# Queries and keys turned by DVE in squares of 32, scores in the array's four row groups

## The chip, the core and the metric

The kernel runs on one core of one Trainium2 chip. The metric is the device time of one execution in microseconds. The kernel before was timed in three executions: median 586.64 us, 584.97 to 586.91 us. A profiled execution (span 578.5 us on the core, TensorE at 0.971 of its full clock on average) gives the times of single instructions. Engines are named as the profile names them: PE is TensorE's matrix multiply, PEld its weight load, DVE is VectorE, ACT is ScalarE, POOL is GpSimd, SP the engine that issues most of the DMA. PSUM is the memory into which PE writes, in banks of 2 KB a partition; SBUF is the working memory of 128 partitions.

## The reference

Two blocks in a row, all in fp32: an attention with a local window and a few global keys, and a layer of eight experts of which each token uses one.

```python
# attention: q, k, v are (4 batches, 8 heads, 768 positions, 64)
scores = q @ k.T / 8                        # per batch and head
keep = (key < n_global) | (0 <= query - key < n_local)     # n_global 8, n_local 96
bias = -slope[h] * dist                     # dist = query - key, or n_local for a far global key
a = softmax(where(keep, scores + bias, -1e9))
x = (a @ v)                                 # heads side by side: 3072 tokens x 512
# router and experts
logits = normed(x) @ normed(expert_emb).T / tau
e = argmax(logits); gate = softmax(logits)[e]
out = gate * (relu(x @ w1[e]) @ w2[e])      # w1 512 x 1024, w2 1024 x 512
```

## The kernel before

The attention goes by groups: a batch and four of its heads (8 groups, two a batch). A group has eight blocks of 96 keys; the keys of a block are seen by its own 96 queries and by the next 96, and 30 further rows hold the possible global keys. So scores of a block are 126 keys by 192 queries a head, keys in the partitions. A step takes two blocks (a group has 4 steps, the kernel 32).

For the scores, PE contracts over the head dimension, so q and k must lie with that dimension in the partitions. They are loaded by tokens: 128 tokens in the partitions, two heads side by side, in runs of 256 bytes. PE turns them with an identity matrix into PSUM, and ACT copies the result out.

```python
def load_tokens(eng, dst, src, b, a, r0, r1):          # two heads (a pair): 256-byte runs
    for e in range(2):
        eng.dma_start(dst[:, r0:r1, e, :],
                      src[b, 2 * a + e].rearrange("(t p) d -> p t d", p=P)[:, r0:r1, :])

def turn(t, i):                                        # a half of q or k of a pair
    src, half = (t.k, t.q)[i // 2], i % 2
    ps = bank()                                        # one of five PSUM banks, shared in turn
    for r in range(3):
        nc.tensor.transpose(ps[:, r * P : (r + 1) * P], src[:, 3 * half + r, :, :], k.ident[:])   # L399
    if i < 2:
        nc.scalar.copy(out=t.kT[:, 4 * half : 4 * half + 4, 0:BLK], ...)     # L401
    else:
        nc.scalar.copy(out=t.qT[:, 3 * half * P : 3 * (half + 1) * P], ...)  # L404
    if i == 0:   # the global keys beside each block
        nc.scalar.copy(out=t.kT[:, :, BLK:ROWS], in_=t.kT[:, 0:1, 0:GLB].to_broadcast([P, NB, GLB]))  # L406

def score(u):                                          # one block u, four heads; L418
    u.sp = [bank() for _ in range(2)]
    for a in range(2):                                 # pair of heads
        for e in range(2):                             # head of the pair: partitions 0-63 or 64-127
            rows = slice(e * D, (e + 1) * D)
            nc.tensor.matmul(u.sp[e][0:ROWS, a * n : (a + 1) * n], lhsT=t.kT[rows, j, 0:ROWS],
                             rhs=t.qT[rows, j * BLK : j * BLK + n], start=True, stop=True)

def grow(u, e):                                        # ACT: exp(scale * scores) into SBUF; L422
    ...
def weigh(u):                                          # DVE: ex = ex * table (bias and mask); L429
    ...
def attend(g, p):                                      # PE: ex x v (L444), sums over the keys (L452)
    ...
    if p % 2:                                          # every second step: out of PSUM
        nc.scalar.copy(out=xd[:, 1, :], ...)           # L457
        nc.vector.tensor_copy(out=xd[:, 0, :], ...)    # L458
        ... den: nc.vector.tensor_copy (L463) for the first group of a batch, nc.vector add (L465) for the second
```

The steps, shortened. Each engine runs its instructions in the order in which they are written here:

```python
for s, (g, p) in enumerate(steps):
    ...                                    # loads of q, k, v two groups ahead
    for u in us: score(u)                  # us: the two blocks of the step
    grow(us[0], 0); grow(us[0], 1)
    weigh(us[0])
    grow(us[1], 0)
    turn(...)                              # turns[s]: two or so a step, of the group ahead
    grow(us[1], 1)
    ...                                    # the other turns; then, for the batch before:
    for hf in active: half_turns(hf)       # PE turns x (L516), DVE scales it (xs, L521), ACT squares it (L526),
                                           # routing: den turned (L483), products lh, lg (L506, L508), small DVE work
    weigh(us[1])
    attend(*steps[s - 1])                  # one step behind
    ...                                    # expert scores (L492), weights of the first experts by DMA
```

After the attention come the experts (L968 is x by w1, L904 by w2), with rows gathered and scattered by GpSimd's indirect DMA (L881, L908).

Of the kernel before, what the change touches and what calls it, by code (L numbers as in the profile page):

```python
# [9 lines left out]
F32 = mybir.dt.float32  # L10
# [10 lines left out]
P = 128  # L21
# [264 lines left out]
def window_table(k, tmp):  # L286

# [33 lines left out]
    for m in range(2):  # L323
        yield
        for e in range(2):
            for a in range(2):
                nc.scalar.activation(k.table[:, m, e, a], rel[:], AF.Exp, scale=-k.slopes[4 * m + 2 * a + e])
# [3 lines left out]
def window_attention(k, ctx):  # L331

# [4 lines left out]
    def pool(name, bufs, **kw):  # L337
# [6 lines left out]
                 for name, n in (("wa_qk", 4), ("wa_tmp", 1)))  # L344
    kt_p, v_p = pool("wa_kt", 4), pool("wa_v", 3)
    ex_p, late_p, const = pool("wa_ex", 6), pool("wa_late", 2), pool("wa_const", 1)
    xd_p, den_p, xs_p, rt_p = pool("wa_xd", 5), pool("wa_den", 3), pool("wa_xs", 2), pool("wa_rt", 2)
    k.junk = const.tile([P, k.DM], F32, name="junk")
    k.table = const.tile([P, 2, 2, 2, 4, BLK], F32, name="table")
# [6 lines left out]
    def new_pair():  # L356
        t = Net()
        t.k = qk_p.tile([P, NT, 2, D], F32, name="k", tag="k")
        t.q = qk_p.tile([P, NT, 2, D], F32, name="q", tag="q")
        t.qT = kt_p.tile([P, S], F32, name="qT", tag="qT")  # L360
        t.kT = kt_p.tile([P, NB, P], F32, name="kT", tag="kT")
        return t

    def load_tokens(eng, dst, src, b, a, r0, r1):

        for e in range(2):
            eng.dma_start(dst[:, r0:r1, e, :],
                          src[b, 2 * a + e].rearrange("(t p) d -> p t d", p=P)[:, r0:r1, :])
# [12 lines left out]
    def open_group(g):  # L381
        g.pairs = [new_pair() for _ in range(2)]
        g.v = v_p.tile([P, 4, NB, D], F32, name="v", tag="v")

    def load_part(g, p):
        if p < 2:
            load_tokens(nc.sync, g.pairs[p].k, k.k, g.b, 2 * g.m + p, 0, NT)
            load_tokens(nc.sync, g.pairs[p].q, k.q, g.b, 2 * g.m + p, 0, NT)
        else:
            load_v(g, (2 * p - 4, 2 * p - 3))  # L390
# [3 lines left out]
    def turn(t, i):  # L394

        src, half = (t.k, t.q)[i // 2], i % 2
        ps = bank()
        for r in range(3):
            nc.tensor.transpose(ps[:, r * P : (r + 1) * P], src[:, 3 * half + r, :, :], k.ident[:])  # L399
        if i < 2:  # L400
            nc.scalar.copy(out=t.kT[:, 4 * half : 4 * half + 4, 0:BLK],  # L401
                           in_=ps[:, 0 : 3 * P].rearrange("d (j c) -> d j c", c=BLK))
        else:
            nc.scalar.copy(out=t.qT[:, 3 * half * P : 3 * (half + 1) * P], in_=ps[:, 0 : 3 * P])  # L404
        if i == 0:
            nc.scalar.copy(out=t.kT[:, :, BLK:ROWS], in_=t.kT[:, 0:1, 0:GLB].to_broadcast([P, NB, GLB]))  # L406

    def score(u):

        j, n = u.j, u.n  # L410
        u.sp = [bank() for _ in range(2)]
        u.ex = (late_p if u.late else ex_p).tile([P, 2, 2, 2 * BLK], F32, name="ex", tag="ex")
        u.ex = u.ex[0:ROWS, :, :, 0:n]
        for a in range(2):
            t = u.g.pairs[a]
            for e in range(2):
                rows = slice(e * D, (e + 1) * D)
                nc.tensor.matmul(u.sp[e][0:ROWS, a * n : (a + 1) * n], lhsT=t.kT[rows, j, 0:ROWS],  # L418
                                 rhs=t.qT[rows, j * BLK : j * BLK + n], start=True, stop=True)

    def grow(u, e):
        nc.scalar.activation(u.ex[:, e], u.sp[e][0:ROWS, 0 : 2 * u.n].rearrange("p (a c) -> p a c", a=2), AF.Exp,  # L422
                             scale=k.scale)
# [766 lines left out]
```

## Time and profile before

| view | what it shows |
|---|---|
| median time | 586.64 us (3 executions) |
| span of the profiled execution | 578.5 us, 9188 instructions |
| PE busy | 548.2 us (95%), 3542 matmuls |
| DVE, ACT busy | 164.5 us (28%), 142.3 us (25%) |
| score matmuls (L418), 64x192 and 64x96 | 512, mean 336 ns |
| turns of q and k on PE (L399) | 96 and 96, mean 299 and 292 ns |
| their copies on ACT (L401, L404) | 32 and 32, mean 498 and 484 ns |
| products with the window's table on DVE (L429), 126x768 | 56, mean 954 ns |
| copies of 128x384 on DVE: xd (L458), den (L463) | 16 and 8, mean 550 and 546 ns |
| DMA packets | 117331, of which 92965 are under 512 bytes |

How to read it: in the profile's lists, a line such as "L418 PE MATMUL pa<-qT,kT 64*126 64x192 f32" is a group of instructions of line 418: the engine, the operation, the tile written and those read, the rows and columns of the array that are used (64 rows, 126 columns), and the moving operand's shape. Matmuls overlap in the array, so their mean durations add up to more than the time they take; the distance between their starts is the cost of one. "Busy" is the time in which at least one instruction ran on that engine. The DMA share is the busy share of the core's 16 DMA engines.

### The profile page before, as it was taken

Reading aid. Unit: us, or ns where it says so; the run is one execution under the profiler, and the core shown is the slowest. Engines: PE = TensorE matmul, PEld = TensorE weight load, DVE = VectorE, ACT = ScalarE, POOL = GpSimd, SP = SyncE. Lnnn points to the kernel's source line nnn. Section 1 sums busy time; section 2 is a strip of 40 time slices with the busy share of each in tenths; the row PEclk is TensorE's granted clock in tenths of the full one; section 3 lists DMA queues with packets and bytes.
Section 4 is the critical chain, followed back from the end, with each engine's and each line's share of the span. In section 5 each row is a group of like instructions: output and inputs, shape, how many; then the busy total and the mean of one; then the engine's idle time right before and its main releaser. Section 6 shows DMA issues by size and latency. Waiting matters only on the chain.

```text
span 578.5 us, 9188 instructions
## 1 busy us (share of the span) xinstructions
PE 548.2 (95%) x3542; PEld 350.8 (61%) x3542; DVE 164.5 (28%) x411; ACT 142.3 (25%) x336; POOL 101.8 (18%) x130
## 2 busy tenths in 40 slices
PE   8899999999989798999999999999999999999980
PEld 8577788787767676757444447556556444645530
DVE  3254666675775412111000110212101110210010
ACT  4575756756643210001001001001001001001100
POOL 2000015013232225140130013030130130110010
PEclk9799999999989898999999999999999999999995
DMA  8999998994246414543460326443461460010000
GB/s 174 194 186 201 258 254 182 256 235 72 74 128 185 126 25 129 189 150 115 177 238 0 123 84 238 158 142 120 160 232 39 159 226 30 16 43 20 2 36 25
DMA packets 117331, 78.11 MB, mean 135 GB/s; under 512 B 92965, under 2 KB 101157, under 8 KB 117169
## 3 DMA queue, kind: packets, MB, share of 16 engines
q1 hardware_dynamic: 109744, 60.72, 40.9%
q0 software_dynamic: 5536, 15.25, 7.4%
q8 instruction: 51, 0.84, 0.6%
q14 instruction: 112, 0.91, 0.5%
q10 hardware_dynamic: 1888, 0.40, 0.4%
HBM read 63.38 MB, written 13.16 MB: 132 GB/s over the span
## 4 chain that ended last, share of the span: by engine, by line
PE 58%; issue 2%; DMA 1%; POOL 1%; DVE 0%; POOLq 0%
PE big L968 27%; PE work L904 25%; PE work L939 3%; PE work L894 2%; DMA xg<-x_dram,ids 1%; POOL xg L881 0%; POOL out_dram L908 0%; POOL meta L245 0%; DVE y L907 0%; POOLq L1004 0%; DVE flags L1018 0%; POOLq L908 0%; POOLq L881 0%
## 5 line engine op out<-in xcount | busy, mean ns | idle before, releaser
L968 PE MATMUL big<-xT,w1t 128*128 128x320 f32 (+5 forms) x512 | 159.0, 472 | 0.0
L904 PE MATMUL work<-w2t,hT 128*128 128x512 f32 x320 | 139.4, 595 | 0.0
L968 PEld LDWEIGHTS big<-xT,w1t 128*128 128x128 f32 x512 | 95.0, 193 | 64.4 <-issue 31.6
L904 PEld LDWEIGHTS work<-w2t,hT 128*128 128x128 f32 x320 | 60.3, 190 | 74.6 <-issue 73.8
L970 ACT ACTIVATE hT<-big 128x640 f32<-128x640 f32 (+5 forms) x32 | 24.9, 777 | 303.7 <-PE big L968 303.7
L429 DVE TENSOR_TENSOR ex<-ex,table 126x768 f32<-126x768 f32 x64 | 57.7, 904 | 57.9 <-ACT ex L422 55.9
L907 DVE TENSOR_SCALAR y<-work,emt 128x512 f32<-128x512 f32 x22 | 16.5, 751 | 156.7 <-PE work L904 150.0
L422 ACT ACTIVATE ex<-pa 126x384 f32<-126x384 f32 (+1 forms) x128 | 53.3, 476 | 28.8 <-PE pa L418 28.8
L908 POOL DMA_INDIRECT out_dram<-y,ids x22 | 21.8, 992 | 185.6 <-DVE y L907 133.1
L895 DVE COPY xT<-work 128x512 f32<-128x512 f32 x32 | 20.1, 683 | 109.9 <-PE work L894 109.9
L418 PE MATMUL pa<-qT,kT 64*126 64x192 f32 (+1 forms) x512 | 50.7, 336 | 0.4 <-ACT ex L422 0.4
L444 PE MATMUL od<-ex,v 126*64 126x192 f32 (+1 forms) x576 | 48.6, 316 | 0.0
L418 PEld LDWEIGHTS pa<-qT,kT 64*126 64x126 f32 x512 | 41.5, 190 | 10.7 <-issue 6.0
L444 PEld LDWEIGHTS od<-ex,v 126*64 126x64 f32 x576 | 36.0, 142 | 8.8 <-issue 4.7
L881 POOL DMA_INDIRECT xg<-x_dram,ids x34 | 33.3, 981 | 23.0 <-issue 15.6
L245 POOL DMA_INDIRECT meta<-mt,slot x24 | 26.3, 1095 | 38.3 <-DVE good L542 7.8
L452 PE MATMUL od<-ex,halves 126*32 126x192 f32 (+1 forms) x576 | 26.9, 310 | 0.0
L943 POOL DMA_INDIRECT out_dram<-y,pids x7 | 7.1, 1015 | 89.3 <-DVE y L942 84.0
L217 POOL TENSOR_TENSOR ss<-ss,half 128x3 f32<-128x3 f32 (+1 forms) x6 | 6.3, 1047 | 93.0 <-ACT junk L526 93.0
L526 ACT ACTIVATE junk<-xs 128x512 f32<-128x512 f32 x24 | 15.2, 632 | 27.1 <-DVE xs L521 22.2
L939 PE MATMUL work<-w2t,hT 128*32 128x128 f32 (+1 forms) x320 | 20.4, 317 | 0.0
L452 PEld LDWEIGHTS od<-ex,halves 126*32 126x32 f32 x576 | 14.9, 111 | 8.8 <-issue 3.6
(143 smaller groups left out, 389.9 us busy)
## 6 DMA issues: line engine op xcount, KB each, us to landing
w1t<-in_moe_w_dram SPq DMA_DIRECT2D x6, 2048.0 KB, 9.5
w2t<-in_moe_w_dram SPq DMA_DIRECT2D x6, 2048.0 KB, 11.5
v<-in_v_dram SPq DMA_DIRECT2D x32, 192.0 KB, 4.7
x_dram<-xs SPq DMA_DIRECT2D x24, 256.0 KB, 2.8
k<-in_k_dram SPq DMA_DIRECT2D x28, 192.0 KB, 4.0
q<-in_q_dram SPq DMA_DIRECT2D x28, 192.0 KB, 4.2
w1t<-in_moe_w_dram SPq DMA_DIRECT2D x32, 128.0 KB, 3.7
w2t<-in_moe_w_dram SPq DMA_DIRECT2D x32, 128.0 KB, 3.7
```

What stands on the lines that cost most here:

```text
L245: i = nc.gpsimd.indirect_dma_start(out=k.meta[:], out_offset=bass.IndirectOffsetOnAxis(ap=slot[:, t : t + 1], axis=0), in_=mt[:, t, :], in ...
L418: nc.tensor.matmul(u.sp[e][0:ROWS, a * n : (a + 1) * n], lhsT=t.kT[rows, j, 0:ROWS], rhs=t.qT[rows, j * BLK : j * BLK + n], start=True, st ...
L422: nc.scalar.activation(u.ex[:, e], u.sp[e][0:ROWS, 0 : 2 * u.n].rearrange("p (a c) -> p a c", a=2), AF.Exp, scale=k.scale)
L429: nc.vector.tensor_tensor(out=exv, in0=exv, in1=tab[:, :, 0 : u.n // BLK, :], op=ALU.mult)
L444: nc.tensor.matmul(g.od[a][e * D : (e + 1) * D, at : at + c1 - c0], lhsT=g.v[0:ROWS, 2 * a + e, u.j, :], rhs=u.ex[:, e, a, c0:c1], start=f ...
L452: nc.tensor.matmul(g.od[2][32 * i : 32 * i + 32, at : at + c1 - c0], lhsT=k.halves[0:ROWS, g.m].rearrange("p i c -> p (i c)"), rhs=u.ex[:, ...
L881: nc.gpsimd.indirect_dma_start(out=xg[:], out_offset=None, in_=k.x_dram[0 : upto or k.N + 1, :], in_offset=bass.IndirectOffsetOnAxis(ap=id ...
L904: nc.tensor.matmul(ps[:], lhsT=hT[:, f, j * P : (j + 1) * P], rhs=w2[:, f, :], start=f == 0, stop=f == k.NF - 1)
L908: nc.gpsimd.indirect_dma_start(out=k.out[:, :], out_offset=bass.IndirectOffsetOnAxis(ap=ids[:, j, 1:2], axis=0), in_=y[:], in_offset=None, ...
L939: nc.tensor.matmul(ps[i * size : (i + 1) * size, 0:m], lhsT=hT[:, f, base : base + size], rhs=w2[:, f, i * m : (i + 1) * m], start=f == 0, ...
L968: nc.tensor.matmul(ps[:, i, 0:w], lhsT=w1[:, c, f * P : (f + 1) * P], rhs=xT[:, c, 0:w], start=c == 0, stop=c == k.NC - 1)
L970: nc.scalar.activation(hT[:, 2 * f2 : 2 * f2 + 2, 0:w], ps[:, :, 0:w], AF.Relu)
```

## The change

What it is for: q and k are no longer turned by PE through PSUM and ACT, but by DVE, from SBUF to SBUF. DVE turns squares of 32 by 32. So q and k are loaded in another layout: a head in each quarter of the partitions (32 partitions), a partition holding three positions of a block of 96 in one run of 768 bytes. A square of 32 then gives 32 values of the head dimension in the partitions. The 64 values of a head are two such halves, which lie side by side in the free dimension (index y), and the scores are the sum of two matmuls of 32 rows that accumulate in PSUM; the four heads lie in four row groups of the array, each with a PSUM bank of its own.

Further: a step's scores now fill four banks at once (two blocks of four heads); the product with the table goes by two heads and both blocks of the step; the copies of xd and of the first den go from DVE to ACT; the turns stand ahead of the step's scores in the program; the order of the first loads and turns is new. Nothing is computed in lower precision, and the experts are untouched.

```diff
-    def load_tokens(eng, dst, src, b, a, r0, r1):
-        for e in range(2):
-            eng.dma_start(dst[:, r0:r1, e, :],
-                          src[b, 2 * a + e].rearrange("(t p) d -> p t d", p=P)[:, r0:r1, :])
+    def load_tokens(eng, dst, src, g, j):        # first group: one block, four heads
+        eng.dma_start(dst[:, j], src[g.b, 4 * g.m : 4 * g.m + 4, j * BLK : (j + 1) * BLK, :]
+                      .rearrange("h (i r) d -> h i (r d)", r=3))
+    def load_head(dst, src, g, h):               # other groups: one head, eight blocks
+        nc.sync.dma_start(dst[32 * h : 32 * h + 32],
+                          src[g.b, 4 * g.m + h].rearrange("(j i r) d -> i j (r d)", j=NB, r=3))
...
-    def turn(t, i):
-        ...                                      # three PE transposes, one ACT copy
+    def turn(g, what, j):
+        src = (g.k if what == "k" else g.q)
+        for b in (j, j + 1):
+            if what == "k":
+                dst = g.kT[:, :, b, 0:BLK].rearrange("p y (i r) -> p r y i", r=3)
+            else:
+                dst = g.qT[:, :, b * BLK : (b + 1) * BLK].rearrange("p y (i r) -> p r y i", r=3)
+            nc.vector.transpose(dst, src[:, b].rearrange("p (r y x) -> p r y x", r=3, y=2))
+        if what == "k" and j == 0:
+            for y in range(2):
+                nc.scalar.copy(out=g.kT[:, y, :, BLK:ROWS], in_=g.kT[:, y, 0:1, 0:GLB].to_broadcast([P, NB, GLB]))
...
+    def score(s, g, us):
+        sp = [bank() for _ in range(4)]
+        ...
+        for i, u in enumerate(us):
+            at = slice(i * 2 * BLK, i * 2 * BLK + u.n)
+            for y in range(2):
+                for h in range(4):
+                    rows = slice(32 * h, 32 * h + 32)
+                    nc.tensor.matmul(sp[h][0:ROWS, at], lhsT=g.kT[rows, y, u.j, 0:ROWS],
+                                     rhs=g.qT[rows, y, u.j * BLK : u.j * BLK + u.n], start=y == 0, stop=y == 1)
+    def grow(t, h):
+        nc.scalar.activation(ex[:, h, :], sp[h][0:ROWS, 0:w], AF.Exp, scale=k.scale)
+    def weigh(t, us, half):                      # heads 2*half and 2*half+1
+        if us[0].j and w == 4 * BLK:
+            ...                                  # one product of 2 x 2 x 192 elements
+        else:
+            for u in us:                         # first and last step of a group: one product a block
+                ...
...
-            nc.vector.tensor_copy(out=xd[:, 0, :], in_=g.od[0][:, 0 : QB * BLK])
+            nc.scalar.copy(out=xd[:, 0, :], in_=g.od[0][:, 0 : QB * BLK])
...
-                nc.vector.tensor_copy(out=den[h][:], in_=g.od[2][:, 0 : QB * BLK])
+                nc.scalar.copy(out=den[h][:], in_=g.od[2][:, 0 : QB * BLK])
...
-    for a in range(2):
-        load_tokens(nc.sync, first.pairs[a].k, k.k, 0, a, 0, 3)
-        load_tokens(nc.scalar, first.pairs[a].q, k.q, 0, a, 0, 3)
+    for j in range(2):
+        load_tokens(nc.sync, first.k, k.k, first, j)
+    for j in range(3):
+        load_tokens(nc.scalar, first.q, k.q, first, j)
...                                              # q3 on the ACT queue, v of the group, then k2..k7 with q4..q7
+    for x in (("k", 0), ("q", 0), ("q", 2)):     # ahead of the table's DVE work
+        turn(first, *x)
...
-            at = [1, 1, 1, 2, 2, 2, 3, 3]        # steps in which group 1 is turned
+            at = [2, 2, 2, 2, 3, 3, 3, 3]
...
-        for u in us:
-            score(u)
-        grow(us[0], 0)
-        grow(us[0], 1)
-        weigh(us[0])
-        grow(us[1], 0)
-        ...                                      # turns
-        grow(us[1], 1)
+        for x in turns[s]:
+            turn(*x)
+        now = score(s, g, us)
+        grow(now, 0)
+        grow(now, 1)
+        weigh(now, us, 0)
+        grow(now, 2)
+        grow(now, 3)
...
-            weigh(us[1])
+            weigh(now, us, 1)                    # at the same place, after the batch before's turns
```

## The prediction, made before the changed kernel was run

> **What bounds the kernel now.** I read the page first (engine shares, the slices, the chain), then the stage table, then the shapes group by group, then the timeline of one step of the attention.
>
> The slices and the chain of the page:
>
> ```profile
> PE   8899999999989798999999999999999999999980
> ...
> DVE  3254666675775412111000110212101110210010
> ACT  4575756756643210001001001001001001001100
> ...
> DMA  8999998994246414543460326443461460010000
> ...
> PE 58%; issue 2%; DMA 1%; POOL 1%; DVE 0%; POOLq 0%
> ```
>
> Each slice is 14.5 us. The first fourteen are the attention and its routing, the rest the experts. The chain holds only the experts: followed in time it begins at 206.8 us, where it meets the last scatters of GpSimd, so it says nothing of the attention. For that, the stage table (columns: length, busy time and instructions of PE, PEld, DVE, ACT, POOL, then the granted clock, the DMA share and GB/s):
>
> ```profile
> 9.60:25.80 16.20, 13.04 (x88) 9.07 (x87) 6.21 (x14) 8.87 (x22) 0.98 (x3) 0.80 1.24 207
> 30.40:138.40 108.00, 107.58 (x1387) 85.52 (x1383) 67.17 (x136) 69.33 (x183) 17.85 (x18) 1.00 1.03 217
> ...
> 224.50:578.00 353.50, 337.96 (x1286) 185.72 (x1286) 41.92 (x107) 24.86 (x32) 54.82 (x56) 0.98 0.32 113
> ```
>
> The rows are the start, the steady attention, and the experts. The score matmuls begin at 30.4 us in step 3 and at 138.4 us in step 24, so 21 steps take 108.0 us, 5.14 us each. In them PE has no hole (107.58 of 108.0), DVE is busy 67.17/21 = 3.20 us a step, ACT 3.30, and the DMA engines are full (share 1.03), though no engine waits for them there. PE in program order is the bound; DVE has 1.94 us of room a step. The experts, 353.5 us, are untouched.
>
> What a step of PE is made of (timeline of one step):
>
> ```profile
> 101.52 1.57 PE L418 MATMUL pa<-qT,kT 64*126 64x192 f32 x16
> 103.02 0.55 PE L399 MATMUL pa<-ident,q 128*128 128x128 f32 x3
> 103.41 0.49 PE L399 MATMUL pa<-ident,k 128*128 128x128 f32 x3
> 103.73 0.60 PE L516 MATMUL pa<-ident,xd 128*128 128x128 f32 x4
> 104.26 1.52 PE L444 MATMUL od<-ex,v 126*64 126x192 f32 x16
> 105.72 0.86 PE L452 MATMUL od<-ex,halves 126*32 126x192 f32 x16
> 106.50 1.57 PE L418 MATMUL pa<-qT,kT 64*126 64x192 f32 x16
> ```
>
> Start differences are the cost, since the durations run into each other: scores 103.02 - 101.52 = 1.50 us, turns of q and k 103.73 - 103.02 = 0.71, the rest 2.77.
>
> **What the Trainium skill says.** (1) "TensorEngine Tiling (Array Packing)", Tiling Modes, Key Properties: tiles of the array load weights and multiply in parallel, and a change of the tiling mode drains the array. The trace agrees: the scores start in pairs 7 ns apart, a new pair each 163 ns; the 32-column sums (L452) in fours each 163 ns; at a change of shape some 0.25 us pass. No run here shows four row groups. (2) "TensorE: Matmul & The Clock Gate", LDWEIGHTS: a load costs by its columns, not its rows. It agrees: 190 ns for 64x126 and 193 for 128x128. (3) "VectorE: DVE Perf Modes", The three transpose paths: DVE turns only squares of 32, 128x128 of bf16 in 311 ns; no run here shows it. (4) "SBUF — State Buffer", Specifications: lines of 16 bytes, each needing two hits for the full rate. The one strided DVE read here agrees: the reduction L508 reads 192 elements 32 bytes apart and takes 505 ns, where L506 takes 358 ns for 192 elements in runs of eight.
>
> **The change part by part, a step (four steps a group).**
>
> *PE, removed:* 24 transposes a group, 6 a step. Inside a run they start 107 to 109 ns apart: 6 x 0.108 = 0.65 us a step. With the steps in which they were the only 128-row work, a change of mode goes as well: I take 0.65 to 0.7.
>
> *PE, scores:* 16 matmuls of 64 rows become 32 of 32 rows with the same 192 columns. If four row groups run at once, a four takes the 163 ns that a pair takes now: 8 x 0.163 = 1.30 us both ways. The 126-column loads double in number. One may take about 0.107 us of its row group (the spacing of the 128-column transposes), under 0.163, if each row group loads beside the others; with two groups they must already overlap, as two in turn would be 0.21. Dispatch: L452 shows 16 matmuls and 16 loads in 0.65 us, 20 ns an instruction, just the rate that 64 instructions in 1.30 us need. So 0.0 us, with a tail of risk. PE's step: 5.14 - 0.65 = 4.49 us.
>
> *DVE, added:* 16 transposes of 128x192 a group, 4 a step. Price of one: 358 ns if an element a cycle (L506), 505 ns if the output, written 12 bytes apart, pays as the read of L508 does. I take 0.41. A duration hides 0.08 us of the next start (L508 at 100.26 takes 0.51, L521 starts at 100.69), so 4 x 0.33 = 1.32 us.
>
> *DVE, weights of the window:* the full-width products stay at 768 elements, but the first step of a group now needs four of 384 (4 x 0.549 = 2.20 for 1.91) and the last two of 384 and two of 192 (2 x 0.549 + 2 x 0.35 = 1.80 for 1.50): 0.59 a group, 0.15 a step.
>
> *DVE, removed:* 16 copies of xd at 0.550 and 8 of den at 0.546 in 32 steps: 13.2/32 = 0.41 us. DVE's step: 3.20 + 1.32 + 0.15 - 0.41 = 4.26 us, 95% of PE's 4.49. DVE goes from 62% to nearly full.
>
> *ACT:* 64 copies at about 0.49 go (31.3 us in all), 24 come (11.4 us at 0.475): 3.30 - 0.62 = 2.7 us. No bound.
>
> *Sum, steady:* were both engines fed perfectly 0.65 us a step would go. But DVE's work is uneven (routing steps have some 17 small operations), transposes stand ahead of the products in its queue, four score banks of five now hang on DVE having read the turned x, and PE waits for the products. I give 0.25 of it back: 4.75 us a step, 0.4 saved over the some 24 steps with turns: 9.6 us.
>
> *Start:* step 2 begins at 25.8 us though step 1 begins at 13.3, since turns of group 1 stand in PE's queue and wait for their q and k (1.5 and 1.3 us), the products for the queue behind; a step then takes about 5. About 7 us is lost. Now PE is free of turns and the first blocks are packets of 768 bytes. But DVE's queue waits for the same data in step 2. I take 4 us.
>
> *DMA:* q and k in the steady stage go from 256-byte packets to a third as many of 768. 68,000 packets of under 512 bytes there, some 60% of them q and k by the sizes of the loads (6144 a group, v 4032), so the full queue becomes looser. Nothing waits for it now, so 0; it is what lets the pace rise.
>
> *End:* xd's copies go one after the other on ACT, +0.5 us before the last routing; in return the wait of 2.3 us for DVE's xd copy at 169 us may shrink. 0.
>
> Sum: 9.6 + 4 = 13.6 us; 586.6 - 13.6 = 573 us. As I lean to a transpose a bit cheaper than 0.41, I say 572.
>
> **The rivals.**
>
> *DVE becomes the bound.* At 0.55 us a transpose DVE's step is 3.20 + 4 x 0.47 + 0.15 - 0.41 = 4.82, and unevenness puts the step at 5.1: nothing gained but the start, 582 to 588 us. For it: the 12-byte stride and L508. Against: writes may be free where reads are not, and the skill's two hits a line are nearly met.
>
> *Four row groups don't run four abreast.* If loads or issue serialize at 60 ns a pair, the scores take 1.9 us and the gain is gone; at 80 ns (today's spacing) 2.6 us, 0.65 a step lost: 600 us or more. For it: the issue rate needed is the highest that the trace shows. Against: L452 keeps it.
>
> *DMA sets the pace.* It is full now. Heads land in 32 partitions each, and if such narrow writes are slower, prefetch falls behind: 575 to 585 us. Against: fewer packets, and loads are issued a group ahead.
>
> *All goes right.* DVE at 0.36 us, PE alone the bound, 0.6 x 24 + 5: 566 us.
>
> **Range and chances.** All right or nearly (560 to 574.9, over 2%): 0.57. DVE or DMA takes part of the gain (574.9 to 598): 0.35. Row groups or queue order fail: 0.08. Range for 8 in 10: 560 to 590.
>
> **What would show it.** Right: no group L399; score matmuls of 32x192 in fours about 163 ns apart, 1.5 us for 32; a DVE transpose group with a mean of 0.36 to 0.45 us, 128 in number; DVE over 85% busy between steps 3 and 24; a step of 4.5 to 4.8 us; the experts still about 354 us. Wrong: a transpose over 0.5 us with PE waiting for the products or for DVE to free a bank; score matmuls spread over more than 2 us; holes in PE for DMA.

## The result: 607.9 us, 3.7% slower, and the profile after

The changed kernel takes 607.94 us (median; 606.64 to 609.69) where the kernel before takes 586.76 (584.97 to 586.91): a ratio of 1.037, 95% interval 1.0336 to 1.0404. Predicted were 572 us and a faster kernel.

First the page of the changed kernel: the slices (15.1 us each) and the engines' shares of the chain.

```profile
PE   7676998798978979899999999999999999999990
...
DVE  3463788488676431211110101111210210200010
ACT  1343465365444431000101100100101001001100
...
PEclk9987999899998888999999999999999999999995
DMA  4599999999313632454346042446055433010000
...
PE 72%; DVE 8%; DMA 7%; ACT 4%; issue 3%; SPq 2%; another core or an unknown queue 1%; POOL 1%; ACTq 0%; DVEq 0%; POOLq 0%
```

PE, at 8 or 9 in the first thirteen slices of the page before, now has sixes and sevens among its first eight. The DMA engines stand at 4 and 5 of 10 in the first two slices, where they were 8 and 9: the start has less DMA work in hand, not more. The chain is long now, and DMA and DVE are in it.

The stage table of the same profile (columns as before: length, busy time and instructions of PE, PEld, DVE, ACT, POOL, then clock, DMA share, GB/s): step 0 to step 2, step 3 to step 24, eight quiet steps in the middle (7 to 15), and the experts.

```profile
11.55:30.73 19.18, 11.63 (x99) 8.13 (x99) 10.22 (x32) 5.64 (x14) 0.06 (x1) 1.00 0.60 127
34.97:159.07 124.10, 107.26 (x1596) 79.80 (x1593) 89.55 (x245) 61.42 (x164) 17.73 (x18) 0.93 1.02 200
65.10:104.68 39.58, 37.51 (x615) 28.32 (x611) 32.97 (x93) 23.27 (x64) 3.75 (x4) 1.00 1.05 227
253.70:605.80 352.10, 335.94 (x1282) 183.83 (x1282) 41.51 (x107) 24.90 (x32) 54.84 (x56) 0.98 0.33 113
```

The 21 steps that took 108.0 us take 124.1. Yet the eight quiet ones take 39.58/8 = 4.95 us each, with the clock at 1.00: faster than before. The experts' 352 us are what they were. So the loss lies in the attention, in stretches.

What the change promised is there. One step of it (timeline), and the new DVE groups by shape (us in all, mean ns, then the idle time before them and what ended it):

```profile
125.66 1.58 PE L417 MATMUL pa<-qT,kT 32*126 32x192 f32 x32
...
126.50 0.69 DVE L402 STREAM_TRANSPOSE kT<-k 128x192 f32<-128x192 f32 x2
127.08 0.65 DVE L402 STREAM_TRANSPOSE qT<-q 128x192 f32<-128x192 f32 x2
...
127.17 0.65 PE L525 MATMUL pa<-ident,xd 128*128 128x128 f32 x4
...
130.68 1.34 PE L417 MATMUL pa<-qT,kT 32*126 32x192 f32 x32
```

```profile
L402 DVE STREAM_TRANSPOSE kT<-k 128x192 f32<-128x192 f32 x64 | 22.6, 407 | 17.5 <-DMA k<-in_k_dram 9.6 <-DMA v<-in_v_dram 7.9
L402 DVE STREAM_TRANSPOSE qT<-q 128x192 f32<-128x192 f32 x64 | 21.9, 393 | 10.9 <-DMA q<-in_q_dram 10.4 <-issue 0.3
```

The scores take 127.17 - 125.66 = 1.51 us, as before; the four row groups run abreast. PE's turns are gone. A DVE transpose takes 0.39 to 0.41 us. But DVE stood 28.4 us before its transposes, all but 0.3 for loads, and its queue is in order: products behind them wait as well. (The 7.9 us under v's name are a wait for k too: by the trace's landings the last head of k is there at 53.6 us, and the transpose begins at 53.8.) The wait also goes another way, through ACT. Steps 4 and 5 (timeline):

```profile
50.27 0.59 PE L417 MATMUL pa<-qT,kT 32*126 32x192 f32 x2
...
53.77 0.70 DVE L402 STREAM_TRANSPOSE kT<-k 128x192 f32<-128x192 f32 x2 [7.92 <-DMA v<-in_v_dram]
54.29 0.69 ACT L405 COPY kT<-kT 128x240 f32<-128x240 f32 x2 [10.50 <-DVE kT L402]
...
54.88 1.63 ACT L424 ACTIVATE ex<-pa 126x384 f32<-126x384 f32 x4
...
55.42 3.68 PE L417 MATMUL pa<-qT,kT 32*126 32x192 f32 x30 [4.56 <-ACT ex L424]
```

ACT's copies of the next group's global keys wait for the transposes, and stand in ACT's queue ahead of step 4's exps, whose scores were done at 48.6 us. The exps then free the banks late, and two of step 5's 32 score matmuls can start while the other 30 wait for 4.6 us. In step 3 the same costs PE 3.2 us. No run moves these copies alone, so how much of the loss would go with them isn't shown.

**Where the time goes.** The profile of before shown above has a span of 578.5 us, below all the timed runs of that kernel; one taken later, beside the experiments, has 587.7, with stalls that the first lacks (they are treated below). The table sets that one against a profile of the changed kernel from the experiments. Each figure is the first score matmul of a step, in us.

| | before | changed | difference |
|---|---|---|---|
| step 2 | 23.32 | 31.06 | +7.7 |
| step 6 | 46.03 | 61.88 | +15.8 |
| step 15 | 91.77 | 104.74 | +13.0 |
| step 16 | 99.00 | 116.80 | +17.8 |
| step 23 | 134.46 | 150.58 | +16.1 |
| step 24 | 146.48 | 159.18 | +12.7 |
| step 31 | 187.78 | 203.02 | +15.2 |
| experts' first product | 234.53 | 253.68 | +19.1 |

So: 7.7 us lost up to step 2, 8.1 more up to step 6, 2.9 and 1.7 won back in steps 6 to 15 and 16 to 23, about 1.4 of stalls (+4.8 and -3.4), 6.5 lost from step 24 to the experts. The profile of before in the table has a hole of its own in step 4 (7.5 us, 4.1 in the first profile, with a wait of 2.1 us for q); against the first profile steps 2 to 6 lose 11.8.

### The profile page after: what moved, and what is told of

Same layout as the page of the kernel before. It is cut to its first block, busy times and chain, and to the rows that moved or that the text cites. A ratio compares the mean times of both kernels' runs of the same rounds, so it can differ in the third digit from the quotient of the medians.

```text
span 605.8 us, 9973 instructions
## 1 busy us (share of the span) xinstructions
PE 548.2 (90%) x3882; PEld 342.9 (57%) x3882; DVE 190.2 (31%) x547; ACT 125.3 (21%) x296; POOL 101.8 (17%) x130
## 4 chain that ended last, share of the span: by engine, by line
PE 72%; DVE 8%; DMA 7%; ACT 4%; issue 3%; SPq 2%; another core or an unknown queue 1%; POOL 1%; ACTq 0%; DVEq 0%; POOLq 0%
PE big L969 26%; PE work L905 24%; PE od L453 5%; PE pa L417 5%; PE work L940 3%; DMA q<-in_q_dram 3%; PE od L461 3%; PE work L895 2%; ACT ex L424 2%; DMA v<-in_v_dram 2%; DVE ex L433 1%; SPq L358 1%; PE pa L598 1%; DVE xs L530 1%; DMA k<-in_k_dram 1%
## 5 line engine op out<-in xcount | busy, mean ns | idle before, releaser
L417 PE MATMUL pa<-qT,kT 32*126 32x192 f32 (+1 forms) x1024 | 61.8, 352 | 18.0 <-ACT ex L424 8.7
L417 PEld LDWEIGHTS pa<-qT,kT 32*126 32x126 f32 x1024 | 49.0, 198 | 31.7 <-issue 12.5
L424 ACT ACTIVATE ex<-pa 126x384 f32<-126x384 f32 (+1 forms) x128 | 50.2, 481 | 41.9 <-PE pa L417 36.1
L453 PE MATMUL od<-ex,v 126*64 126x192 f32 (+1 forms) x576 | 54.3, 338 | 2.9 <-DVE ex L433 2.6
L453 PEld LDWEIGHTS od<-ex,v 126*64 126x64 f32 x576 | 39.3, 154 | 14.9 <-issue 5.3
L438 DVE TENSOR_TENSOR ex<-ex,table 126x384 f32<-126x384 f32 x64 | 29.1, 497 | 20.4 <-ACT ex L424 20.4
L433 DVE TENSOR_TENSOR ex<-ex,table 126x768 f32<-126x768 f32 x32 | 29.6, 940 | 16.2 <-ACT ex L424 15.4
L461 PE MATMUL od<-ex,halves 126*32 126x192 f32 (+1 forms) x576 | 29.6, 320 | 1.0 <-issue 1.0
L402 DVE STREAM_TRANSPOSE kT<-k 128x192 f32<-128x192 f32 x64 | 22.6, 407 | 17.5 <-DMA k<-in_k_dram 9.6
L402 DVE STREAM_TRANSPOSE qT<-q 128x192 f32<-128x192 f32 x64 | 21.9, 393 | 10.9 <-DMA q<-in_q_dram 10.4
L535 ACT ACTIVATE junk<-xs 128x512 f32<-128x512 f32 x24 | 15.1, 631 | 38.4 <-DVE xs L530 25.7
```

Of the source, the lines that this page charges most:

```text
L402: nc.vector.transpose(dst, src[:, b].rearrange("p (r y x) -> p r y x", r=3, y=2))
L417: nc.tensor.matmul(sp[h][0:ROWS, at], lhsT=g.kT[rows, y, u.j, 0:ROWS], rhs=g.qT[rows, y, u.j * BLK : u.j * BLK + u.n], start=y == 0, stop= ...
L424: nc.scalar.activation(ex[:, h, :], sp[h][0:ROWS, 0:w], AF.Exp, scale=k.scale)
L433: nc.vector.tensor_tensor(out=exv, in0=exv, in1=tab, op=ALU.mult)
L438: nc.vector.tensor_tensor(out=exv, in0=exv, in1=tab[:, :, kind :: 3 - kind][:, :, 0 : u.n // BLK], op=ALU.mult)
L453: nc.tensor.matmul(g.od[a][e * D : (e + 1) * D, at : at + c1 - c0], lhsT=g.v[0:ROWS, 2 * a + e, u.j, :], rhs=u.ex[:, 2 * a + e, c0:c1], st ...
```

## The experiments

The theory at first: loads make the loss, those of the start by running on few engines, those of the steady stage by being narrow. Rivals: DVE's queue order; DVE too slow. Ratios are to the kernel before on the same chip at the same time.

### Loads: narrow or wide (e1), the first ones (e2), none (e3), heads crossed (e4)

e1, wide:
```diff
-        nc.sync.dma_start(dst[32 * h : 32 * h + 32],
-                          src[...].rearrange("(j i r) d -> i j (r d)", j=NB, r=3))
+        nc.sync.dma_start(dst[:, h::4],
+                          src[...].rearrange("(j i r) d -> i j (r d)", j=2, r=3))
```


> Each load of a head in groups 1 to 7 writes 128 partitions (32 tokens' thirds from each of four quarters of the head) instead of 32, with the same bytes, the same number of loads and the same 768-byte packets; the rows then stand in the wrong places, so the output isn't the reference's, but every instruction and wait is the same. Theory 'narrow writes' (16 engines crowd into 32 partitions): packets fall from 66 ns to 40-48 ns, the waits of the DVE transposes for k, q and v at 31 to 54 us shrink, the hole-and-half-clock stretch there goes, 592-600 us (8 to 16 less than the change's 608). Rival 'a 768-byte packet costs what its bytes cost' (memory side is the limit): packets stay at 60 ns or more and the time within 2 us of 608.

Ratio 1.0263 (1.0222 to 1.0304), 603.6 us. The experts are reached at 244.8 us, 9 earlier than in the changed kernel; their own stage is 3.7 us longer, probably as the wrong rows are routed otherwise. The queue of q, k, v and weights from 50 to 150 us (packets, MB, share of 16 engines), changed kernel and e1:

```profile
q1 hardware_dynamic: 38995, 20.84, 102.9%
```

```profile
q1 hardware_dynamic: 39936, 21.08, 85.3%
```

More bytes in less engine time. By the packet records from 70 to 150 us a 768-byte packet has a mean of 66 ns in the changed kernel and 42 in e1. The Trainium skill, "SBUF — State Buffer", Door 1: The DMA port swizzle, says that 32 partitions reach only 8 of the 16 ports; these two means agree. Steps 2 to 6 take 18.1 us in place of 31.1. So the theory held for the packets and the holes, and the rival fell; the time is outside the 592 to 600 us expected, by about what the experts take longer.

e2, the first loads by head:
```diff
-    for j in range(2):
-        load_tokens(nc.sync, first.k, k.k, first, j)       # [4 heads, 32, 192] -> 128 partitions
+    for h in range(4):
+        load_rows_of(nc.sync, first.k, k.k, first, h, 0, 2)  # [32, 2 blocks, 192] -> 32 partitions
```
(q the same with blocks 0 to 3; the rest after v.)

> Only the first group's loads of q and k differ: one load per head over several blocks (slowest dimension 32 on both sides) instead of one per block over four heads (slowest dimension 4 at the source). Theory 'the first loads run on 4 engines': 104 GB/s in 0-12 us and 83 GB/s in 12-24 us rise to 150 or more, step 2 begins at 26-27 us instead of 30.7, the queue behind moves up, 598-603 us. Rival 'the start is set by the table and by the DVE queue': step 2 within 1 us of 30.7, 606-609 us.

Ratio 1.0168 (1.0126 to 1.0209), 598.0 us. DMA from 12 to 24 us in 40 slices, changed kernel and then e2:

```profile
DMA  9899963332232222222222222222223222232448
GB/s 202 169 208 224 203 131 62 73 61 69 90 90 72 92 90 87 84 92 87 82 82 87 84 85 82 82 87 87 82 82 90 79 87 82 82 87 87 109 123 220
```

```profile
DMA  9999999999659989999999999999999999999999
GB/s 197 205 231 215 213 202 223 202 201 211 133 135 220 277 218 230 225 207 187 187 169 184 174 197 190 189 210 205 210 200 192 179 197 174 187 177 191 173 174 189
```

A quarter of the engines' time and some 83 GB/s became nearly all of it and some 197: the block loads, whose source's outer dimension is 4 heads, ran on a quarter of the engines. The Trainium skill, "DMA: Bandwidth & Descriptors", Why a DMA increments its semaphore by 16 and not by 1, gives the rule: the largest number up to 16 that divides the outermost dimension of both sides. Here that is 4, and the trace agrees. Step 2 begins at 28.5 us (2.3 earlier; 26 to 27 was expected), step 6 at 52.0 (9.8 earlier), the experts 11 us earlier: the slow first loads held up the loads behind them more than the start itself. Of the edits that keep every load, this one gains most.

e3, none:
```diff
-        g.k = qk_p.tile(...); g.q = qk_p.tile(...)
+        g.k, g.q = first.k, first.q            # for groups 1 to 7, and no load_head at all
```


> No q or k is loaded for groups 1 to 7; their transposes read the first group's q and k (output not the reference's, all other work and all of v's loads are there). Theory 'loads': DVE never waits for k or q, the steady steps take 4.6-4.9 us from step 3 to step 23, 576-585 us, less than the kernel before. Rival 'the DVE queue' (transposes ahead of products, products behind routing, whatever the loads do): holes stay, 598 us or more. A tail (step 23 to the experts) still 6-10 us longer than before would show that part to be of DVE's order and not of the loads.

Ratio 1.0185 (1.0127 to 1.0244), 597.7 us: the theory's 576 to 585 is missed by 13 us. The holes of steps 3 to 6 do go (step 6 at 46.2 us, 61.8 in the changed kernel), so the loads are their cause; 15.4 us of this lie after step 2. But the first loads are still slow here, step 16 is 12.7 us after step 15, and from step 23 to the experts it takes 102.9 us (103.2 in the changed kernel). So the tail is not of the loads; that it is of DVE's order, as the text has it, does not follow from this run.

e4, e2 with q's heads shifted by two:
```diff
-                load_head(g.q, k.q, g, h)
+                load_head(g.q, k.q, g, (h + 2) % 4)
```


> Full computation. The first loads per head as in the run of the first loads alone, q's heads in the order 2, 3, 0, 1, and in the steady loads each k of head h is followed by the q of head h+2 instead of h, so that neighbouring transfers go to both halves of the partitions. Theory 'narrow writes, both halves can be written at once': packets 45-55 ns, 590-597 us. Rival 'one queue, one transfer after another': packets stay at 62-66 ns, and only the gain of the first loads is seen, 598-603 us.

Ratio 1.0117 (1.0076 to 1.0158), 595.6 us. Packets from 70 to 150 us: 54 ns, where e2 has 65. Neighbouring transfers to both halves cost less a packet, though not 42. The time is in the range expected, but a gain from the crossing is not shown: the experts are reached at 242.8 us, in e2 at 242.5, and the two ratios' intervals overlap.

### A wait for the wrong block (e5, e6)

Step 0 of e4 (timeline):

```profile
11.55 1.02 PE L422 MATMUL pa<-qT,kT 32*126 32x192 f32 x8
...
15.32 0.70 DVE L407 STREAM_TRANSPOSE kT<-k 128x192 f32<-128x192 f32 x2 [2.77 <-DMA emb<-in_moe_expert_emb_dram]
...
16.16 4.21 PE L422 MATMUL pa<-qT,kT 32*126 32x192 f32 x30 [3.59 <-DVE kT L407]
```

The second half of the contraction of block 0 waits for the transposes of k's blocks 2 and 3, which it does not read. They stand ahead of it in the program, and their writes, with both halves in one access of kT[:, :, b], enclose the place that it reads (that this enclosing makes the wait is argued from the program; that the order does is what the edit shows). The edit, in e5 to the changed kernel and in e6 to e4:

```diff
-        for x in turns[s]:
-            turn(*x)
         now = score(s, g, us)
+        for x in turns[s]:
+            turn(*x)
```


> The changed kernel with one edit: in each step the transposes stand after the score matmuls in program order, not before them; the DVE queue itself is the same. Theory 'a wait for the wrong block': step 0's second half of the contraction stands waiting for the transposes of blocks 2 and 3, which it doesn't read (the last 28 score matmuls of step 0 began at 16.1 us with the faster first loads, 0.14 us after that transpose, 4.1 us after the first four began to end), and in step 26 the same (0.8 us). Then step 0's exps start 3 to 6 us earlier, step 2 begins at 26-28 us instead of 30.7, 601-605 us against 608. Rival 'step 0 waits for its own data or for the table': step 2 within 1 us of 30.7, time within 2 us of 608.

> The run with first loads per head and heads crossed (595.6 us) with the same edit: transposes after the score matmuls. Theory 'a wait for the wrong block': step 0's exps begin at 13-14 us instead of 18.4, step 2 at 23-25 us instead of 28.4, 590-593 us. Rival 'own data or the table': 594-597 us.

In e6 the same place:

```profile
11.55 2.94 PE L422 MATMUL pa<-qT,kT 32*126 32x192 f32 x32
...
14.51 0.87 ACT L429 ACTIVATE ex<-pa 126x384 f32<-126x384 f32 x2 [7.70 <-PE pa L422]
```

The wait is gone, the exps come 3.9 us earlier, step 2 at 24.2 (e5: 27.6) as expected, 4.2 us before e4's 28.3 (e5: 3.1 before the changed kernel's 30.7). The time did not follow: e5 1.0423 (1.0376 to 1.0470), e6 1.0114 (1.0062 to 1.0166), no better than the kernels they were made from. (Their 603.6 and 585.2 us are no more than was expected, but the kernel before took 579.7 beside them.) In e5 step 6 begins at 61.7 us, in the changed kernel at 61.8: what the start gains, the loads of the next groups take back. A real false wait, worth nothing while another wait stands behind it.

### Order in the queues (e7, e8, e9, e9b), and two repeats

e7 puts 24 tiny copies on ACT before step 0 (the stall, below); e8 adds:
```diff
+        for x in turns[s]:                     # at the end of the step, after weigh(now, us, 1)
+            if x[0] is not first: turn(*x)
```


> The previous one, with 24 tiny copies on ACT (one element a partition) put in where ACT stands idle before step 0. In every run with the change so far ACT stood still 5.7 us before step 15's exps, with its inputs ready for 3 us or more, until 1.0 us after the last of GpSimd's six scatters; those exps are about ACT's 128th instruction. Theory 'ACT's instructions ran out there (a fetch of 128 falls into the scatters)': with 24 more before it the 128th falls into step 12 or 13, ahead of the scatters, the stall is gone or under 1 us and the time 5-7 us less than the previous run. Rival 'whatever ACT has next waits for the scatters (or the scatters hold up ACT)': the stall stays at 5-6 us before step 15's exps and the time is the same or 1-2 us more.

> The previous one, with the transposes of groups 1 to 7 put at the end of each step's DVE work, after the products (the first group's stay where they are). Theory 'transposes hold up the products': PE's waits for products and exps in the steps with routing (steps 23 to 31) shrink, 3-6 us less than the previous run. Rival 'order doesn't matter, DVE has room': within 2 us of the previous run; the tail from step 23 to the experts stays near 102 us.

e7: 1.0092 (1.0062 to 1.0123). The stall was absent in this group of runs, e6 included, so e7 says nothing of its cause. e8: 1.0305 (1.0268 to 1.0342), 12 us slower than e7 where 3 to 6 faster was expected. From step 6 to step 23 it needs 88.8 us and e6 82.5. Transposes ahead of the products are the better order.

> The changed kernel once more, beside the next ones on one chip, for the stall of 5.7 us of ACT before step 15's exps (seen in the five profiles with transposes before the scores, all of other chips than the three with them after, which show none). Theory 'the stall belongs to the order of the instructions': it is there again, 15th to 16th step 12 us. Rival 'it belongs to the chip': it is absent here, and the step takes 5.8-6.2 us.

> The run with loads per head, crossed heads and transposes after the scores once more, beside the changed kernel on one chip. If all three causes (first loads, narrow loads, wait for the wrong block) are real: ratio to the changed kernel 0.965-0.980, of which the stall, if it is of the order of instructions, is 6 us. If the earlier comparison across chips misled: above 0.985.

The changed kernel again 1.0404 (1.034 to 1.0468), e6 beside it 1.0105 (1.0042 to 1.0168): 593.05/609.18 = 0.9735, inside the 0.965 to 0.980 expected. In these runs e6 had the stall as well (step 15 to 16 12.6 us), so the order of the instructions is not its cause.

```diff
-    busy(24)
+    busy(14)                                   # e9 and e9b; also k's blocks 2, 3 ahead of v, group 1 turned after the products
-            at = [... (0, 0, 1, 1, 1, 2, 2, 2)]
+            at = [... (0, 0, 1, 2, 1, 4, 4, 4)]  # e9 alone: the last group's pieces later
```


> The previous one with four more edits: 14 warm-up matmuls on PE at the start, as many as the kernel before has, instead of 24 (step 0's scores began at 11.55 us in every run, when the 24 ended, with q and k turned by 7.9); the first group's k of blocks 2 and 3 loaded ahead of v; group 1's transposes after the products; and five of the last group's eight pieces later (k of blocks 2, 3 a step, the last three to step 28, with q's and k's buffers freed two steps later), as DVE was full from 148 to 158 us in steps 25 and 26 and idle from 159 to 165. Theory 'start and tail were lost to order alone': scores from 8-9 us, step 2 at 20-22 us, step 27 to 28 in 5-7 us instead of 11, 574-580 us where the previous run has 585 and at or under the kernel before. Rival 'the half clock and the loads come back elsewhere': within 3 us of the previous run.

> The same without the last of the four edits (the last group's pieces where the change puts them). Theory 'DVE's full stretch in steps 25 and 26 costs the half clock': 3-6 us slower than the run with it. Rival 'the tail is set by the routing chain': within 2 us of it.

e9 1.0070 (1.0048 to 1.0091), e9b 1.0122 (1.0064 to 1.0179), e6 beside them 1.0105. Scores begin at 7.4 us in place of 11.55, but step 2 at 24.0 and 23.0, no earlier than the 22.8 of e6 beside them: the start's end was not the scores. The later pieces do shorten steps 27 to 31 (23.8 us; 30.7 in e9b), and half of that is lost before the experts (3.7 us remain). Only e9's 3.4 us against e9b look like a gain (the intervals overlap a little); the expected 574 to 580 us were not reached, and e9 is 2.5 us under e6, as the rival had it.

### What is left without narrow loads (e10, e11), and the stall (r_before, r_pad)

e10, made from e6, gives each partition 24 running rows of a head, so that heads and partitions fold into one outer dimension of 128; a transpose then writes every 24th token:
```diff
+            nc.sync.dma_start(dst[...][:, rows],   # 12 rows of 256 bytes running, two halves, groups 1 to 6
+                src[g.b, 4*g.m : 4*g.m+4].rearrange("h (i c) d -> (h i) c d", i=32)[:, rows])
...
+                dst = g.qT[:].rearrange("p y (i c) -> p c y i", c=24)[:, 3 * b : 3 * b + 3]
```


> Full computation: the run with loads per head, crossed heads and transposes after the scores, with q and k of groups 1 to 6 loaded as 24 rows running (two halves of 12 rows, 3 KB) into each of 128 partitions, 2 transfers for a tensor and group where there were 4, and turned with an output step of 96 bytes where it was 12. Theory 'the loads are what is left': no wait of the transposes for k or q at steps 4 to 6, DMA share at 50-150 us under 0.85, 5-10 us less than the run it is made from, at or under the kernel before (ratio 0.990-1.003). Rival 'the wider output step costs DVE what the loads give': transposes take 0.45 us or more and the ratio stays at 1.005-1.015.

> First loads per head, transposes after the scores, and no q and k loads at all for groups 1 to 7 (their transposes read the first group's; output not the reference's, all other work there). What the change would be worth if loads cost nothing. Theory 'loads are what is left': steps 3 to 23 at 4.75-4.95 us each without a hole of over 2 us (the stall of step 15 apart), the experts reached 5-10 us earlier than in the run it is made from. Rival 'DVE and the tail': experts reached within 3 us of it.

e10: 588.61 us, ratio 1.0004 (0.9985 to 1.0023), the best version of the study: the kernel before is equalled, not beaten. Even this is in part luck: beside it the kernel before had the stalls treated below, while e10's own profile has none of ACT (its step 15 takes 8.0 us). e12 below, which is e10 but for its tail, has the same 8.0 us, and beside a kernel before without stalls its ratio is 1.0081. Step 6 begins at 42.1 us (e6: 45.8 and, repeated, 49.6), so the loads' part was right; e10 also moves the copy of the global keys from the first piece of k to the last, and its share in this is not separated. The rival was right too. The transposes of e10 by shape:

```profile
L417 DVE STREAM_TRANSPOSE qT<-q 128x192 f32<-128x192 f32 x64 | 31.8, 593 | 2.1 <-DMA q<-in_q_dram 2.1
...
L417 DVE STREAM_TRANSPOSE kT<-k 128x192 f32<-128x192 f32 x64 | 25.6, 475 | 8.4 <-PE pa L432 3.7 <-DMA tau_sb<-in_moe_tau_dram 2.9 <-DMA k<-in_k_dram 1.8
```

Waits for k and q fell from 20 us in the changed kernel to 4 (9 in e6), but with an output step of 96 bytes in groups 1 to 6 the mean of all transposes is 0.48 us (k) and 0.59 (q), and in these groups alone 0.50 and 0.66. e11, with no load of q and k and the old step: 1.0059 (1.0038 to 1.0080), of which 4 us are a longer expert stage of the wrong rows. So even without these loads (v's and the first group's are there) the change wins nothing: experts at 235.7 us, the kernel before beside it at 234.5.

> The kernel before, profiled on the same chip as the next three. Theory 'the stall is the change's': no step of it is longer than in the first profile, span about 578.5 us. Rival 'the chip's, whatever the kernel': somewhere a stall of 5-8 us of PE or ACT that the first profile lacks, span 584-587 us (only if this chip is one of those with the stall).

> The run with 24 tiny ACT copies early, once more, on this chip. If the chip shows the stall in the next two: theory 'ACT's instruction fetch' has no stall at step 15 here (step 15 to 16 5.8 us); rival 'scatters hold up ACT' has it (12 us).

The stall first. A repeat of the changed kernel (timeline), and the waits of r_pad from 90 to 104 us (us in all, times, longest):

```profile
108.89 0.96 POOL L245 DMA_INDIRECT meta<-mt,slot  x1 [0.30 <-issue]
...
110.86 1.32 ACT L424 ACTIVATE ex<-pa 126x288 f32<-126x288 f32 x4 [5.77 <-remote]
```

```profile
ACT ex L429 <- remote: 5.8, 1, 5.8
```

ACT's inputs were complete at about 107.5 us, and its exps begin 1.0 us after GpSimd's sixth scatter ends, in every run that has the stall. With 24 more ACT instructions ahead of it, it stays where it was: a fetch at the 128th instruction is not the cause. And the kernel before has it too, in r_before in step 23, beside its six scatters (waits from 134 to 147 us):

```profile
DVE ex L429 <- issue: 2.8, 2, 2.1
PEld pa L399 <- issue: 2.3, 1, 2.3
PE pa L399 <- issue: 2.0, 1, 2.0
```

Its step 23 takes 12.0 us and 6.2 in the first profile, its span is 587.7 us. The stalls come in some groups of runs and not in others with the same kernel; where they are absent the kernel before has a median of 580 or 581 us, where they are present 587 to 589. They weigh on both kernels and are not what the change costs. What holds ACT there is open.

### The tail, and the copies moved to ACT (e12, e13)

e12 is e10 with the last group's pieces later, as in e9, and the last xd copy on DVE; e13 is e10 with
```diff
-            nc.scalar.copy(out=xd[:, 0, :], in_=g.od[0][:, 0 : QB * BLK])
+            nc.vector.tensor_copy(out=xd[:, 0, :], in_=g.od[0][:, 0 : QB * BLK])
```
and the same for den.

> The run with long loads with its tail changed alone: of the last group's eight pieces to be turned, k's second moves one step later, the last three from step 26 to step 28 (q's and k's buffers freed two steps later), and the last copy of xd's first half goes to DVE beside ACT's. Theory 'DVE's full stretch in steps 25 and 26 costs a wait, a half clock and so the gain': steps 26 to 30 3-6 us shorter than the 27.6 us of the run it is made from, the experts reached 3-5 us earlier, ratio to the kernel before 0.990-0.997. Rival 'the end waits for the routing chain': what steps 26 to 30 gain is lost again before the experts, ratio 0.998-1.003.

> The run with long loads with one part of the change undone: the copies of xd's first half and of the first sums are DVE's again (0.41 us a step by the first profile). Theory 'DVE has little room and the copies had to go': DVE's busy time a step rises from 4.2 to 4.6 us, PE waits for products, 3-8 us slower than the run it is made from. Rival 'DVE has room, ACT's two copies in a row only lengthen the way to the routing': within 1 us or up to 2 us faster.

e12: 1.0081 (1.0050 to 1.0111); steps 27 to 31 take 28.1 us (e10: 27.6). Neither text holds: no gain there at all, so the tail isn't explained by these pieces. (e10 was measured beside a kernel before with stalls, e12 without: their ratios are not to be set against each other.) e13, beside e12: 1.0239 (1.0206 to 1.0272). From step 7 to step 23, e12 and then e13:

```profile
46.16:130.09 83.93, 75.47 (x1226) 56.58 (x1222) 73.87 (x184) 46.03 (x125) 12.11 (x12) 1.00 0.86 216
```

```profile
46.54:138.28 91.74, 80.86 (x1225) 59.59 (x1222) 80.12 (x196) 41.40 (x112) 11.93 (x12) 0.94 0.80 201
```

DVE's work grows by 6.3 us (12 copies) and the stretch by 7.8: 7.6 of it in steps 7, 11, 15 and 19. DVE, 88% busy in e12, had no room for them. So with these slower transposes the copies had to go to ACT; with the change's own no run shows it.

## Why the prediction was wrong, by its own steps

The sum had 13.6 us saved; 19.1 were lost up to the experts. Of the difference 11.7 us are the start, 8.1 the DMA, 5.0 the steady step, 6.5 the end and 1.4 the stalls.

**Right.** PE's transposes: the time from the first matmul of each of their runs to the first of the next run was 13.4 us in steps 6 to 23 of before, 0.74 a step; 0.65 to 0.7 was said. Scores: 1.51 us, 0.0 more. DVE transpose: 0.393 and 0.407 us, 0.41 said, which was a guess between two readings of other operations. DVE's step: 32.97/8 = 4.12 us in the quiet stretch, 4.26 said; ACT's 2.9, 2.7 said. The rivals on DVE's price and on the row groups fell. Two readings were off without harm: small packets from 25 to 140 us are 67,072, not 68,000, and the weight loads of 64x126 and 128x128 that agreed (190 and 193 ns) leave out those of the turns, 128x128 as well, with 148 to 152 ns.

**The start, "I take 4": wrong in sign.** It cost 7.7 us. The step counted packets and their size and never asked on how many engines a load runs: the four heads as outer dimension left a quarter of them (e2: 2.3 us at step 2, 11 at the experts). Nor did it ask what stands ahead of step 0's scores: transposes of blocks that they don't read (e6: 4.2 us at step 2). With both mended step 2 begins at 22.8 us, where before has 23.3, and in the other pair of profiles at 24.2 and 25.8: of the 4 us, 0.5 to 1.6 came.

**DMA, "so the full queue becomes looser ... so 0": the largest error of reasoning.** A packet three times as long was taken to cost less by the byte. Written into 32 partitions it costs 66 ns, three times the 21 of the 256-byte packets in the same stretch of before; the queue stayed at a share of 1.03, DVE now waited for it, and 8.1 us went in steps 2 to 6. The slow first loads have a part in this: with them mended (e2) steps 2 to 6 take 23.6 us, with wide loads in the other groups (e1) 18.1, in the changed kernel 31.1. "Loads are issued a group ahead" didn't help: by the program group 2's k may start only when the first group's has been turned, and its first transposes need all four heads of it. These loads were issued from 40.8 us on, and the last head of k landed at 53.6. The rival "DMA sets the pace" had named just this, "heads land in 32 partitions each", and gave it 575 to 585 us: it left out that the wait is passed on, by DVE's queue to the products, by ACT's queue to the exps and so to PE, and by PE's holes to its clock. Two stretches of the first profile of the changed kernel, half clock in both:

```profile
39.70:46.50 6.80, 6.54 (x70) 5.26 (x70) 6.11 (x18) 4.09 (x12) 0.71 (x2) 0.50 0.95 172
53.40:60.20 6.80, 4.78 (x38) 4.09 (x40) 5.23 (x13) 4.97 (x13) 0.00 (x0) 0.50 0.99 185
```

**Steady step, "4.75": the term given back was mis-sized.** From step 6 to step 24, of before and of e6, without stalls in either:

```profile
44.75:138.37 93.62, 93.62 (x1203) 74.78 (x1200) 60.12 (x125) 60.07 (x158) 17.18 (x16) 1.00 1.01 223
```

```profile
45.76:134.01 88.25, 84.04 (x1384) 63.41 (x1380) 74.70 (x205) 50.13 (x134) 16.34 (x16) 1.00 1.02 224
```

93.62/18 = 5.20 us and 88.25/18 = 4.90: 0.30 a step, not 0.40, and PE has 4.2 us of holes where it had none. Of the 13.4 us of turns, 8.0 come back: 3.2 in the weighted sums (PE waits for products for 2.6), 3.0 at the turns of xd, 1.2 at the scores. The 3.0 are 0.23 us for each of 13 runs of xd's turns, about what the prediction read at a change of shape; that the turns of q and k had paid this for them is argued, not tested. In the changed kernel 2.9 + 1.7 us were won over 16 steps, where the sum had 9.6 over 24.

**End, "0": about 6.5 us lost from step 24 on.** In the table's two profiles 2.5 of them go up to step 31 and 3.9 after it. PE's holes grow from 10.4 to 15.4 us and its busy time by 1.5, though its turns are gone: after step 31 its mean clock is 0.87, where before has 0.91. In e6, where the time goes (timeline):

```profile
153.03 1.56 PE L422 MATMUL pa<-qT,kT 32*126 32x192 f32 x26 [1.35 <-DVE lh L520]
...
156.50 0.40 PE L210 MATMUL pa<-oh,prefix 128*128 128x24 f32 x2 [1.32 <-ACT ex L429]
...
158.00 2.83 PE L458 MATMUL od<-ex,v 126*64 126x192 f32 x16
...
162.20 2.29 PE L422 MATMUL pa<-qT,kT 32*126 32x192 f32 x32
```

PE waits for a bank that DVE frees late, then for the exps, and then runs at half clock (2.83 us for sums that take 1.20 elsewhere). That DVE, full with the routing, the split products and the last group's transposes, starts it is argued from this; e9 bears it out by 3.7 us, e12 does not. The rest of the tail is open.

## What to carry to other kernels

Before a load's layout is changed for longer packets, work out how many engines its outer dimension leaves and how many partitions it writes at once; longer packets gained nothing here, and few engines or few partitions cost more than the change could win. An engine with room that gets transposes of freshly loaded data also gets the loads' waits, and passes them to all that stands behind in its queue; a small copy that reads the transposes' output does the same in the queue of another engine. And a false wait is worth removing only when the next wait behind it is not as late.

## What the runs showed of the hardware that was not expected

- A 768-byte packet had a mean of 66 ns into 32 partitions, 54 with neighbouring transfers into both halves of the partitions, 42 into 128.
- A DVE transpose of 128x192 in 4 bytes took 0.39 to 0.41 us with an output step of 12 bytes, 0.50 (k) and 0.66 (q) in the groups that had a step of 96 (e10).
- PE's clock fell to half in a hole or just after it (holes of 3.2 and 4.6 us in the changed kernel's steps 3 and 5) and stayed there for 6.8 us both times, elsewhere for 3.4 (at 111.4 and 183.1 us); so such a hole cost up to 3.4 us more.
- In some groups of runs, in both kernels, engines stood while GpSimd's six scatters ran, with nothing in the trace to wait for: ACT for 5.8 us in the changed kernel, PE and DVE for some 2 us in the kernel before.
